# Attention feeding a gated feed-forward block: attention matmuls as array tiles, exp and gate phases per batch, one program order

## The chip, the cores and the metric

One core of a Trainium2 chip. The metric is the device time of one execution in microseconds (us). Executions of one kernel mostly lie within 0.7% of each other. The engines are named as in the profile: PE is TensorE (matmuls), ACT is ScalarE, DVE is VectorE, POOL is GpSimd, which also issues all loads here; PEld is the loading of weights on TensorE. The granted clock is the share of the full TensorE clock that the chip allows at a time.

## The reference, cut to what matters

Eight batches, eight heads, 576 queries, 16 "beacon" keys that everyone sees in front of 576 causal keys, head size 64. The result, 4608 tokens of 512, goes through a gated block of width 1536.

```python
k_all = concat([beacon_k, k]); v_all = concat([beacon_v, v])
a = softmax(0.125 * q @ k_all.T, causal mask on the last 576 keys)
x = (a @ v_all).transpose(0, 2, 1, 3).reshape(4608, 512)
out = (gelu(x @ w_gate) * (x @ w_val)) @ w_out
```

## The kernel before

Heads are handled in pairs, so one 128-row tile holds both. Scores come out transposed (keys on rows). Value matmuls use the exp tile as the stationary operand and give 65 columns, the last of them the row sum. One unit of feed-forward work is put between the key tiles.

```python
# scores: full 128 rows; the other head's half of the queries is zero
nc.tensor.matmul(scs[hi][0:kr, 0:width], kT_sb[0:P, jj*P : jj*P+kr],
                 qT_sb[hi][0:P, s_lo : s_lo+width], start=True, stop=not diag)
...  # diagonal tile: add the mask with an identity matmul, then Exp per head
nc.tensor.matmul(x_ps[0:N, hi, :], expT[0:kr, hi, off : off+N], v_sb[0:kr, jj, 2*m+hi, :], ...)
...  # reciprocal, scale, transpose back into xT_sb
# main loop
for jj in range(N_KT):
    attn_qk_tile(jj, qT_sb, kT_sb, expT)
    try_emit_ffn(tokens_written, 1)
    if pending: attn_av_chunk(*pending.pop(0))
...
```

In the feed-forward part the gate goes through Tanh on ACT and two DVE instructions; every product of 128x512 is one matmul, 1296 of them.

The softmax here doesn't subtract the row's maximum and nothing guards it: scores larger than these inputs give would overflow.

## Time and profile before

| | before |
|---|---|
| time, median of 2 | 484.74 us (484.02 to 485.46) |
| PE busy | 433.9 us of 481.2 |
| one batch of attention and one 512-token chunk | 51.1 us |

First the page: busy time, share of the span and instruction count of PE, then rows of the 40-slice view (tenths busy; PEclk is the granted clock in tenths).

```profile
PE 433.9 (90%) x3384; PEld 238.6 (50%) x3440; DVE 267.6 (56%) x1020; ACT 265.9 (55%) x625; POOL 125.0 (26%) x174
PE   2488699999998999989999999999998999999994
PEclk9999899999999999999999999999999999999998
```

The table of stages of the same kernel: stretch, its length, then busy us (and instructions) of PE, PEld, DVE, ACT and POOL, granted clock, DMA share and GB/s.

```profile
80.00:440.00 360.00, 344.02 (x2736) 189.91 (x2783) 214.50 (x829) 209.49 (x497) 66.17 (x86) 1.00 0.47 46
```

The chain of waits of the same kernel (start, length, what): the first output matmuls of chunks (the third is left out).

```profile
88.09 2.32 PE o_ps L334 x10
...
138.30 2.59 PE o_ps L334 x12
...
241.28 2.59 PE o_ps L334 x12
```

PE is what bounds the kernel from 80 us on: 344 of 360 us busy, at full clock. A chunk and a batch take 51.1 us ((241.28 - 88.09)/3). Twelve 128x512 matmuls take 2.59 us, so the 144 of a chunk take 31.1 us, and four pairs of attention the other 20.0.

### The profile page before, as it was taken

The numbers are of one execution on the slowest core, as the hardware profiler recorded it, in microseconds if no ns is written. First come the engines' busy times: TensorE is split into PE (matmuls) and PEld (weight loads), VectorE is DVE, ScalarE is ACT, GpSimd is POOL, SyncE is SP. The second block draws the span as 40 slices with busy tenths as digits, with TensorE's granted clock in tenths as the row PEclk, the third lists the DMA queues.
The fourth block names the chain that finished last, engine by engine and source line by source line (L and its number), as shares of the span: only waits on it lengthen the run. The fifth ranks groups of instructions, "written<-read, shape, count | busy, mean of one in ns | idle before, by whom it ended". The sixth has DMA issues, their size and how long they took to land.

```text
span 481.2 us, 8884 instructions
## 1 busy us (share of the span) xinstructions
PE 433.9 (90%) x3384; PEld 238.6 (50%) x3440; DVE 267.6 (56%) x1020; ACT 265.9 (55%) x625; POOL 125.0 (26%) x174
## 2 busy tenths in 40 slices
PE   2488699999998999989999999999998999999994
PEld 0255455555555555555555455555555554544441
DVE  0056387347843786268625783488437762782850
ACT  2388546665556755584657556655566554332321
POOL 9998129933430415040330300000000000000000
PEclk9999899999999999999999999999999999999998
DMA  4999999998592809054392800200020000200202
GB/s 28 85 119 163 206 173 126 131 157 52 36 67 80 59 2 101 0 111 29 24 78 89 52 1 0 89 1 1 1 89 1 1 0 1 90 0 1 87 1 87
DMA packets 122491, 29.16 MB, mean 61 GB/s; under 512 B 115280, under 2 KB 116816, under 8 KB 122448
## 3 DMA queue, kind: packets, MB, share of 16 engines
q0 software_dynamic: 117696, 19.15, 54.3%
q1 hardware_dynamic: 4752, 9.44, 5.2%
q8 instruction: 27, 0.44, 0.4%
q14 instruction: 16, 0.13, 0.1%
HBM read 38.27 MB, written 9.44 MB: 99 GB/s over the span
## 4 chain that ended last, share of the span: by engine, by line
PE 66%; ACT 13%; POOL 8%; DVE 6%; DMA 4%; issue 2%; ACTq 0%; POOLq 0%
PE o_ps L334 19%; PE g_ps L297 17%; PE v_ps L306 15%; ACT expT L222 4%; DVE p_sb L316 4%; DMA wv_sb<-in_moe_w_val_dram 4%; PE x_full L240 4%; ACT th_sb L314 4%; POOL v_sb L118 3%; POOL k_sb L118 3%; POOL q_sb L118 2%; PE xTf L261 1%; ACT qT0B_121 L176 1%; ACT kT_sb L188 1%; DVE hT_sb L319 1%
## 5 line engine op out<-in xcount | busy, mean ns | idle before, releaser
L297 PE MATMUL g_ps<-xT_sb,wg_sb 128*128 128x512 bf16 x394 | 109.2, 379 | 7.7 <-DMA wg_sb<-in_moe_w_gate_dram 2.3
L306 PE MATMUL v_ps<-xT_sb,wv_sb 128*128 128x512 bf16 x421 | 111.0, 379 | 1.3 <-DMA wv_sb<-in_moe_w_val_dram 0.9
L314 ACT ACTIVATE th_sb<-g_ps 128x512 bf16<-128x512 f32 x108 | 64.4, 598 | 78.4 <-PE g_ps L297 53.8
L316 DVE SCALAR_TENSOR_TENSOR p_sb<-th_sb,g_ps 128x512 bf16<-128x512 bf16 x108 | 74.1, 687 | 51.7 <-ACT th_sb L314 51.5
L334 PE MATMUL o_ps<-wo_sb,hT_sb 128*128 128x512 bf16 x426 | 98.0, 379 | 0.9 <-DVE xT_sb L262 0.6
L249 DVE RECIPROCAL rec_sb<-x_full 128x1 f32<-128x1 f32 (+2 forms) x320 | 36.5, 155 | 99.0 <-PE x_full L240 84.7
L251 DVE TENSOR_SCALAR xn_sb<-x_full,rec_sb 128x64 bf16<-128x64 f32 (+2 forms) x320 | 76.1, 278 | 0.0
L319 DVE SCALAR_TENSOR_TENSOR hT_sb<-p_sb,v_ps 128x512 bf16<-128x512 bf16 x108 | 73.2, 679 | 4.3 <-PE v_ps L306 2.5
L306 PEld LDWEIGHTS <-wv_sb 128*128 128x128 bf16 x432 | 41.6, 98 | 47.9 <-DMA wv_sb<-in_moe_w_val_dram 1.4
L297 PEld LDWEIGHTS <-wg_sb 128*128 128x128 bf16 x432 | 41.2, 97 | 47.6 <-issue 13.7
L334 PEld LDWEIGHTS <-hT_sb 128*128 128x128 bf16 x432 | 40.6, 98 | 46.0 <-issue 1.6
L240 PE MATMUL x_full<-v_sb,expT 128*128 128x65 bf16 (+3 forms) x960 | 60.4, 198 | 0.0
L240 PEld LDWEIGHTS <-expT 128*128 128x128 bf16 (+3 forms) x960 | 51.0, 108 | 17.7 <-issue 0.6
L341 ACT COPY o_sb<-o_ps 128x512 f32<-128x512 f32 x36 | 21.1, 585 | 68.4 <-PE o_ps L334 68.4
L262 DVE COPY xT_sb<-xTf 128x128 bf16<-128x128 bf16 (+2 forms) x160 | 34.4, 215 | 41.9 <-PE xTf L261 41.9
L118 POOL DMA_DIRECT2D q_sb<-in_q_dram x45 | 37.4, 893 | 47.5 <-PE qT_ps L170 47.5
L118 POOL DMA_DIRECT2D k_sb<-in_k_dram x45 | 37.4, 900 | 16.3 <-DMA wo_sb<-in_moe_w_out_dram 8.3
L216 PEld LDWEIGHTS <-ident 128*128 128x128 bf16 (+1 forms) x320 | 29.6, 103 | 17.7 <-issue 7.7
L261 PE MATMUL xTf<-ident,xn_sb 128*128 128x128 bf16 (+2 forms) x160 | 34.8, 217 | 2.6 <-DVE xn_sb L251 2.2
L118 POOL DMA_DIRECT2D v_sb<-in_v_dram x45 | 37.0, 869 | 0.0
L206 PEld LDWEIGHTS <-kT_sb 128*128 128x128 bf16 (+1 forms) x384 | 33.1, 104 | 6.3 <-issue 3.5
L261 PEld LDWEIGHTS <-xn_sb 128*128 128x128 bf16 (+2 forms) x160 | 15.6, 97 | 27.6 <-DVE xn_sb L251 17.0
(1121 smaller groups left out, 488.2 us busy)
## 6 DMA issues: line engine op xcount, KB each, us to landing
out_dram<-o_sb SPq DMA_DIRECT2D x9, 1024.0 KB, 4.4
q_sb<-in_q_dram POOLq DMA_DIRECT2D x28, 128.0 KB, 5.8
k_sb<-in_k_dram POOLq DMA_DIRECT2D x21, 128.0 KB, 4.4
v_sb<-in_v_dram POOLq DMA_DIRECT2D x21, 128.0 KB, 4.8
wg_sb<-in_moe_w_gate_dram POOLq DMA_DIRECT2D x1, 1536.0 KB, 11.5
wv_sb<-in_moe_w_val_dram POOLq DMA_DIRECT2D x1, 1536.0 KB, 18.1
wo_sb<-in_moe_w_out_dram POOLq DMA_DIRECT2D x1, 1536.0 KB, 26.1
k_sb<-in_k_dram POOLq DMA_DIRECT2D x7, 112.0 KB, 4.6
```

The lines of the kernel that those rows point to most:

```text
L118: nc.gpsimd.dma_start(out=out_ap, in_=in_ap)
L240: nc.tensor.matmul(x_ps[0:N, hi, :], expT[0:kr, hi, off : off + N], v_sb[0:kr, jj, 2 * m + hi, :], start=(idx == 0), stop=(idx == ntiles - 1),
L249: nc.vector.reciprocal(rec_sb[0:N, hi : hi + 1], x_ps[0:N, hi, 64:65])
L251: nc.vector.tensor_scalar(out=xn_sb[0:N, 64 * hi : 64 * hi + 64], in0=x_ps[0:N, hi, 0:64], scalar1=rec_sb[0:N, hi : hi + 1], scalar2=None, ...
L261: nc.tensor.transpose(xT_ps, xn_sb[0:N, :], ident[0:N, 0:N])
L262: nc.vector.tensor_copy(xT_sb[:, m, n0 : n0 + N], xT_ps)
L297: nc.tensor.matmul(g_ps, wg_sb[:, kk, fi * P : (fi + 1) * P], xT_sb[:, kk, n0 : n0 + N_TOK_CHUNK], start=(kk == 0), stop=(kk == K_CHUNKS - 1),
L306: nc.tensor.matmul(v_ps, wv_sb[:, kk, fi * P : (fi + 1) * P], xT_sb[:, kk, n0 : n0 + N_TOK_CHUNK], start=(kk == 0), stop=(kk == K_CHUNKS - 1),
L314: nc.scalar.activation(th_sb, g_ps, ACT.Tanh, scale=GELU_TANH_SCALE)
L316: nc.vector.scalar_tensor_tensor(out=p_sb, in0=th_sb, scalar=1.0, in1=g_ps, op0=ALU.add, op1=ALU.mult)
L319: nc.vector.scalar_tensor_tensor(out=hT_sb[:, fi, :], in0=p_sb, scalar=0.5, in1=v_ps, op0=ALU.mult, op1=ALU.mult,)
L334: nc.tensor.matmul(o_ps, hT_sb[:, fi, ti * P : (ti + 1) * P], wo_sb[:, fi, :], start=(fi == 0), stop=(fi == F_TILES - 1),)
```

## The change

The intent: let PE run two heads side by side (scores on two row halves of the array, values and row sums on two column halves), drop the transposes of x and the mask matmuls, give ACT and DVE fewer and larger instructions, and use the exact Gelu. The kernel loads one table set for Exp and Ln and another for Gelu (16 loads in its trace, 1 in that of the kernel before), so each batch has an exp phase, with the previous chunk's output matmuls filled in, and a gate/value phase. Everything is pinned in program order (`keep`).

```diff
-    scores on 128 rows with zero halves, mask matmul, 12 Exps per pair
+    r = slice(64 * hi, 64 * hi + 64)
+    mm(s_ps[:, hi, col : col + w], qkT[r, 1, t*P : (t+1)*P], qkT[r, 0, s_lo : s_lo + w], True, True)
+    ...
+    act(expT[:, :, o : o + w], s_ps[:, :, 0:w], ACT.Exp, scale=QK_SCALE)   # 4 per pair
+    keep(nc.gpsimd.affine_select(out=d, in_=d, ...))                        # mask, on Pool
-    values: 65 columns, exp tile stationary; reciprocal, scale, transpose, copy
+    mm(x_ps[64*hi : 64*hi+64, base+q0 : base+q1],
+       v_sb[0:kr, t, 2*m+hi, :] if base == X0 else ones[0:kr, :], expT[0:kr, hi, ...], ...)
+    act(ln_sb, x_ps[:, Z0 : Z0 + S], ACT.Ln)
+    act(rec_sb, ln_sb, ACT.Exp, scale=-1.0)
+    keep(nc.vector.tensor_tensor(out=xT_sb[:, m, ...], in0=x_ps[:, X0 : X0 + S], in1=rec_sb, op=ALU.mult))
+    psum_s bufs=2 (scores, transposes, gate/value), psum_x bufs=1, psum_o bufs=1
...
+    for b in range(B):
+        keep(nc.scalar.preload_act_table_set(SET_EXP))
+        for m in range(NPAIR):
+            n = 3 if m < NPAIR - 1 else 2
+            scores(b, m, 0); o(n)                  # o(n): n output matmuls of chunk b-1
+            scores(b, m, 1); av(m - 1, 0, 2); o(n)
+            scores(b, m, 2)
+            if m < NPAIR - 1: transpose_pair(b, m + 1)
+            av(m - 1, 4, 1, 3)
+            scores(b, m, 3)
+            if m: normalize(b, m - 1)
+            o(2 * n if m < NPAIR - 1 else 0)
+            if b == 0 and m < 3: (gate/value weights 1, weights 2, load_batch(1))[m]
+        av(NPAIR - 1, *AV_ORDER); normalize(b, NPAIR - 1)
+        if b + 1 < B: transpose_pair(b + 1, 0)
+        o(8)
+        keep(nc.scalar.preload_act_table_set(SET_GELU))
+        for fi in range(F_TILES):
+            gate_val(b, fi)
+            if fi == 0:
+                if b == 0: load_out_w(); load_batch(2)
+                if b + 3 < B: load_batch(b + 3)
...
```

(Several lines of the diff are joined or cut here.) In `out_mms`, each group of 12 output matmuls ends with a DVE copy of `o_ps`, which has one buffer.

## The prediction

> **What bounds the kernel now.** TensorE. The page gives PE 433.9 us busy of 481.2 (90%); DVE 56%, ACT 55%. In the table of stages PE is 94 to 97% busy from 80 to 440 us; the only poor part is the first 60 us (35.6 us busy), where Pool issues 51 loads one by one (the Pool timeline runs without a gap from 1.8 to 46.8 us). In the chain of waits the output matmuls of successive 512-token chunks start at 88.1, 138.3, 189.8, 241.3, 292.4 us: one chunk and one batch of attention take 51.3 us.
>
> **Terms, from the trace.** Twelve 128x512 matmuls take 2.59 us, so 0.216 us each. The feed-forward part has 1296: 280 us, unchanged. Per chunk that is 31.1 us, so four head pairs of attention cost 20.2 us of the 51.3.
>
> **Removed:** the mask matmuls, the zero-padded halves of the score matmuls, 160 transposes of x with copies, DVE reciprocal and scale (36.5 + 76.1 us), DVE copy of x (34.4), Tanh's extra DVE step (74.1), small ACT instructions (four wide Exps per pair for twelve). DVE and ACT become much lighter, but neither is the limit.
>
> **Added on PE:** values and row sums stream 2x1664 columns per head instead of 65-column matmuls that cost only about 0.04 us each. If the column tiles run in pairs this is 1.4 us per pair plus small-matmul overhead (1.6 to 2.1 us, estimate), scores 0.8, transposes 0.6: about 3 to 3.5 us per pair, against about 4 of issue time now. The Trainium skill, "TensorEngine Tiling (Array Packing)", Key Properties, says a change of tiling mode drains the array; no view of before shows it. There are some ten changes per pair; I take 0 to 0.12 us each.
>
> **Moved, and decisive.** In the exp phase everything stands in program order, o_ps and x_ps have one buffer, and VectorE gets the normalizing multiply before the o_ps copy. Each pair ends: last scores, Exp (0.52), Ln (0.65), Exp (0.65), multiply (0.76), o_ps copy (0.6), about 3.6 us with latencies (sizes scaled from the 598 ns and 687 ns for 512 elements), against 1.7 us of PE work to cover it. I expect PE to wait about 2 us twice per batch for the o_ps copy, and about 3 us before the fourth pair's values. Exp phase: 31 to 36 us per batch; gate/value phase 20.8 us (PE-bound, Gelu and multiply hide). So the period is 52 to 57 us against 51.3: the PE saving is given back as waits.
>
> **Ends.** The first gate phase starts at about 57 us (51.8 before): the mask selects now queue on Pool behind 17 loads of the next batch at 0.8 us each. Batch 1 may lose 5 us to the same queue. Tail after the eighth gate phase: 31 + 10.4 + 5 us.
>
> Sum: 57 + 20.8 + 7 x 53 + 46 = 495 us. **Predicted 495 us, 460 to 530.** Faster 0.24, same 0.28, slower 0.48.
>
> **What would show it.** PE busy falls to 75 to 80%; PE idle before the first output matmul of pairs 2 and 3 released by the o_ps copy (about 2 us each), and before the fourth pair's value matmuls released by the multiply (3 us); gate phases of 20.8 us with PE full; two value matmuls on different column halves starting within a few ns; in batch 0, value matmuls waiting for Pool's selects; Pool below its former share late, busy early.
>
> **What would make it wrong.** If column tiles do not overlap, add 1.4 us per pair (45 us). If mode changes are free and the waits are shorter than I estimate, the period falls to 46 us and the time to 445. Extra table loads between Exp and Ln would add 1.28 us each (the one load in the trace).

## The result, and the profile after

525.18 us (524.96 to 525.40, 2 runs) against 484.74: slower, ratio 1.084 (95% interval 1.080 to 1.088). Ratios in this document are not quite the ratios of the medians quoted.

The page of the changed kernel, the same lines:

```profile
PE 421.1 (80%) x3104; PEld 208.2 (40%) x3152; DVE 147.0 (28%) x214; ACT 233.4 (45%) x316; POOL 185.1 (35%) x326
PE   2373796869976998779887988699769977899985
PEclk9996699899999899979998999899999999799999
```

PE has fallen from 90% to 80% of a longer span. DVE went from 267.6 to 147.0 us and ACT from 265.9 to 233.4: savings on engines that were not the limit. The PEclk row has more and deeper dips (down to 6) than before, where it has one 8 and the end.

The chain of waits, with the first long piece of successive gate/value phases:

```profile
119.81 9.06 PE gv_ps L132 x42
...
175.41 9.06 PE gv_ps L132 x42
...
232.19 9.06 PE gv_ps L132 x42
...
287.79 9.06 PE gv_ps L132 x42
```

From one to the next it is 55.6, 56.8 and 55.6 us (mean of six periods up to 453.47: 55.6) against 51.1 before. The table of stages for one gate/value phase and one exp phase (columns as above):

```profile
119.80:140.80 21.00, 20.89 (x98) 9.30 (x98) 8.30 (x12) 6.80 (x12) 6.51 (x9) 1.00 0.92 69
140.80:175.40 34.60, 26.44 (x277) 14.28 (x280) 8.30 (x12) 21.41 (x27) 14.59 (x29) 0.95 0.35 42
```

The gate/value phase is full of PE work. The exp phase has 26.4 us of PE work in 34.6 us. Where the other 8 us go is seen in the timeline at the end of one pair (start, length, engine, instruction, and in brackets the idle time before it and what ended it; here and below, weight loads and other lines that the reading does not need are left out):

```profile
264.49 0.26 PE L132 MATMUL s_ps<-qkT_110 64*128 64x208 bf16 x2
264.69 1.47 PE L132 MATMUL o_ps<-wo_sb,hT_sb 128*128 128x512 bf16 x6
264.80 0.52 ACT L135 ACTIVATE expT<-s_ps 128x416 bf16<-128x416 f32 x1 [0.66 <-PE s_ps L132]
265.21 0.64 ACT L135 ACTIVATE ln_sb<-x_ps 128x576 f32<-128x576 f32 x1
265.88 0.68 ACT L135 ACTIVATE rec_sb<-ln_sb 128x576 f32<-128x576 f32 x1
266.09 0.39 PE L132 MATMUL s_ps<-qkT_108 64*128 64x512 bf16 x2
...
266.60 0.76 DVE L223 TENSOR_TENSOR xT_sb<-x_ps,rec_sb 128x576 bf16<-128x576 f32 x1 [2.01 <-ACT rec_sb L135]
267.27 0.68 DVE L272 COPY o_sb<-o_ps 128x512 f32<-128x512 f32 x1
268.01 0.81 PE L132 MATMUL o_ps<-wo_sb,hT_sb 128*128 128x512 bf16 x3 [1.53 <-DVE o_sb L272]
```

The six output matmuls have been done since 266.16, so the copy of `o_ps` could run from then on. But the multiply stands before it in program order and waits for Exp, Ln and Exp on ACT: DVE stays idle for another 0.44 us (the last part of its 2.01 us), then multiplies, and the copy starts at 267.27, 1.1 us late. PE, which has done the first scores of the next pair meanwhile, waits 1.53 us for the copy. The waits of PE in the changed kernel that matter here (total us, times, longest):

```profile
PE o_ps L132 <- DVE o_sb L272: 28.1, 25, 1.5
PE x_ps L132 <- DVE xT_sb L223: 22.0, 9, 2.7
PE x_ps L132 <- POOL expT L180: 14.4, 3, 10.2
...
PE s_ps L132 <- ACT expT L135: 6.1, 18, 0.7
...
PE t_ps L146 <- ACT expT L135: 3.4, 7, 0.5
```

The second line is the fourth pair, whose value matmuls wait 2.66 us for the multiply that frees `x_ps`. The third is mostly one wait in batch 0, in the timeline there:

```profile
50.79 4.19 POOL L108 DMA_DIRECT2D v_sb_102<-in_v_dram  x5 [0.37 <-issue]
54.95 1.76 POOL L180 TENSOR_SCALAR_AFFINE_SELECT expT<-expT 128x224 bf16<-128x224 bf16 x5
55.43 0.69 PE L132 MATMUL x_ps<-expT,v_sb_98 128*64 128x496 bf16 x4 [10.21 <-POOL expT L180]
```

Pool issues all 17 loads of batch 1 before the mask selects that the fourth pair needs. The last two lines of the waits are for the most part the table load at the start of each exp phase, in the timeline of batch 4:

```profile
252.94 0.60 ACT L135 ACTIVATE ge_sb<-gv_ps 128x512 bf16<-128x512 f32 x1 [1.13 <-PE gv_ps L132]
253.56 1.28 ACT L294 ACT_TABLE_LOAD   x1
254.85 2.72 ACT L135 ACTIVATE expT<-s_ps 128x1024 bf16<-128x1024 f32 x3
255.93 0.37 PE L132 MATMUL s_ps<-qkT_108 64*128 64x464 bf16 x2 [0.47 <-ACT expT L135]
256.79 0.42 PE L146 MATMUL t_ps<-ident,q_sb_100 128*128 128x128 bf16 x5 [0.49 <-ACT expT L135]
```

And the table of stages around the 2.66 us wait of that batch shows a cost that no wait shows: the granted clock (the number before the last two).

```profile
279.50:282.20 2.70, 0.06 (x2) 0.00 (x0) 0.76 (x1) 1.82 (x4) 2.34 (x4) 1.00 0.00 0
282.20:283.20 1.00, 0.98 (x12) 0.68 (x14) 0.00 (x0) 0.00 (x0) 1.00 (x2) 0.64 1.23 79
283.20:284.20 1.00, 1.00 (x18) 0.86 (x16) 0.00 (x0) 0.00 (x0) 1.00 (x3) 0.50 1.54 98
284.20:285.20 1.00, 1.00 (x17) 0.79 (x14) 0.00 (x0) 0.17 (x1) 1.00 (x2) 0.50 1.79 114
285.20:286.20 1.00, 0.94 (x11) 0.88 (x10) 0.00 (x0) 0.97 (x2) 1.00 (x3) 0.65 2.35 150
```

After the wait PE works for about 3.4 us at half clock, which loses 0.36 + 0.50 + 0.50 + 0.35 = 1.7 us. That an idle PE falls to half clock is in the Trainium skill, "TensorE: Matmul & The Clock Gate", Part 1; it speaks of idle windows of about 3.4 us, and here 2.66 us were enough. They were not always: in this profile six of the seven waits of 2.66 us were followed by half clock (about 3.4 us four times, 6.8 us twice), in the control's profile (e0) five of seven, in that of e1 four. None of the fourteen waits of 1.53 us was, within 5 us. The kernel before has one such case, after a wait of 2.28 us.

### The profile page after: what moved, and what is told of

The parts are those of the page before. It is cut to its first block, busy times and chain, and to the rows that moved or that the text cites. A ratio compares the mean times of both kernels' runs of the same rounds, so it can differ in the third digit from the quotient of the medians.

```text
span 523.7 us, 7515 instructions
## 1 busy us (share of the span) xinstructions
PE 421.1 (80%) x3104; PEld 208.2 (40%) x3152; DVE 147.0 (28%) x214; ACT 233.4 (45%) x316; POOL 185.1 (35%) x326
## 4 chain that ended last, share of the span: by engine, by line
PE 62%; ACT 12%; POOL 11%; DVE 5%; DMA 5%; issue 4%; DVEq 0%; POOLq 0%
PE gv_ps L132 32%; PE o_ps L132 13%; PE x_ps L132 11%; ACT expT L135 5%; PE s_ps L132 4%; DVE o_sb L272 3%; PE t_ps L146 3%; ACT rec_sb L135 3%; POOL v_sb_98 L108 2%; DMA wo_sb<-in_moe_w_out_dram 2%; ACT ln_sb L135 2%; POOL k_sb_97 L108 2%; DMA wv_sb<-in_moe_w_val_dram 2%; DVE xT_sb L223 2%; POOL q_sb_96 L108 2%
## 5 line engine op out<-in xcount | busy, mean ns | idle before, releaser
L135 ACT ACTIVATE expT<-s_ps 128x1024 bf16<-128x1024 f32 (+3 forms) x128 | 108.5, 864 | 96.3 <-PE s_ps L132 95.8
L180 POOL TENSOR_SCALAR_AFFINE_SELECT expT<-expT 128x256 bf16<-128x256 bf16 (+2 forms) x160 | 59.9, 404 | 252.2 <-ACT expT L135 251.3
L132 PE MATMUL o_ps<-wo_sb,hT_sb 128*128 128x512 bf16 x401 | 106.5, 388 | 32.9 <-DVE o_sb L272 28.1
L135 ACT ACTIVATE ge_sb<-gv_ps 128x512 bf16<-128x512 f32 x108 | 64.5, 597 | 137.3 <-PE gv_ps L132 137.3
L132 PE MATMUL gv_ps<-xT_sb,wg_sb 128*128 128x512 bf16 x422 | 110.7, 380 | 0.6 <-issue 0.2
L132 PE MATMUL gv_ps<-xT_sb,wv_sb 128*128 128x512 bf16 x425 | 109.4, 379 | 0.4
L251 DVE TENSOR_TENSOR hT_sb<-gv_ps,ge_sb 128x512 bf16<-128x512 f32 x108 | 74.7, 692 | 123.2 <-ACT ge_sb L135 123.2
L132 PE MATMUL x_ps<-expT,ones 128*64 128x144 bf16 (+5 forms) x576 | 54.2, 275 | 0.0
L132 PE MATMUL x_ps<-expT,v_sb_98 128*64 128x80 bf16 (+5 forms) x216 | 21.1, 284 | 20.6 <-POOL expT L180 11.9
L272 DVE COPY o_sb<-o_ps 128x512 f32<-128x512 f32 x36 | 24.7, 685 | 21.4 <-PE o_ps L132 21.4
L132 PE MATMUL s_ps<-qkT_108 64*128 64x512 bf16 (+2 forms) x192 | 23.4, 295 | 8.5 <-ACT expT L135 5.3
L132 PEld LDWEIGHTS <-ones 128*64 128x64 bf16 (+1 forms) x576 | 27.1, 127 | 6.4 <-issue 1.5
L132 PE MATMUL x_ps<-expT,v_sb_102 128*64 128x80 bf16 (+5 forms) x216 | 19.7, 272 | 10.5 <-DVE xT_sb L223 8.0
L132 PE MATMUL s_ps<-qkT_110 64*128 64x512 bf16 (+2 forms) x192 | 23.3, 297 | 0.8 <-ACT expT L135 0.8
```

Of the source, the lines that this page charges most:

```text
L132: keep(nc.tensor.matmul(out_ap, lhsT, rhs, start=start, stop=stop, **kw))
L135: keep(nc.scalar.activation(out_ap, in_ap, func, **kw))
L180: nc.gpsimd.affine_select(out=d, in_=d, pattern=[[0, 2], [1, DIAG[t]]], compare_op=ALU.is_ge, fill=0.0, base=NB if t == 0 else 0, channel_ ...
L251: nc.vector.tensor_tensor(out=h_of[ci][:, fi, :], in0=gv_ps[:, 1, :], in1=ge_sb, op=ALU.mult)
L272: keep(nc.vector.tensor_copy(o_sb[:, ti, :], o_ps))
```

## The experiments

My theory after the result: the PE work did get shorter, and the program order gave it back in separate waits. The rival: PE's own work is what got long (tiles that do not overlap, or changes of tiling), and the waits only show slack. Each of the first three runs mends one wait. Unless said otherwise an edit is to the changed kernel, whose time as a control was 525.47 us (4 runs; ratio to before 1.082). The experiments ran on three chips (e1 to e4, e5 to e8, the rest). The kernel before ran in each, with medians of 484.87, 484.39 and 485.49 us, so the ratios compare best, and a difference of medians between calls carries about 1 us of that.

### e1_copy_first

```diff
-            if m:
-                normalize(b, m - 1)
             o(2 * n if m < NPAIR - 1 else 0)
+            if m:
+                normalize(b, m - 1)
```

> Edit: the output matmuls that end a pair are written before the normalization, so VectorE copies o_ps before it does the normalizing multiply. Theory (waits on single-buffered PSUM tiles in program order eat the gain): the two waits of 1.53 us per batch before the next pair's output matmuls shrink to about 0.6 us (o_ps copy starts when the sixth matmul lands), the multiply comes 0.3 us later and hurts nobody; 2.1 us x 7 batches = 15 us less, about 510 us. Rival (TensorE's own work is longer than thought: tiling changes, small matmuls, cold clock): the wait moves to another place and the time stays within 3 us of 525.

Measured: 507.11 us (4 runs), ratio to before 1.045, so 18 us less than the control. PE's wait for the copy fell from 28.1 to 13.2 us in all; in the timeline the 1.53 us became:

```profile
258.30 0.81 PE L132 MATMUL o_ps<-wo_sb,hT_sb 128*128 128x512 bf16 x3 [0.46 <-DVE o_sb L272]
```

The order of two DVE instructions cost 3.5% of the kernel. The rival of this run fell. The waits account for 15 of the 18 us. Part of the rest is clock: after its seven waits of 2.66 us PE was at half clock for 17 us in all in the profile of e1 and for 24 us in the control's, which is worth up to 3.4 us. Whether the edit or chance did that is not shown.

### e2_fill_fourth

```diff
+        o(8)
         av(NPAIR - 1, *AV_ORDER)
         normalize(b, NPAIR - 1)
         if b + 1 < B:
             transpose_pair(b + 1, 0)
-        o(8)
```

> Edit: the eight output matmuls that follow the fourth pair's value matmuls are put before them, into the 2.66 us wait for the normalizing multiply. Theory: the wait falls to about 0.9 us, the TensorE clock stays granted in full and the 36 value matmuls take 2.1 us where they took 2.8; a new wait of about 1.1 us appears at the start of the gate phase, which now has less work to hide the last normalization. Net about 1.3 us x 7 = 9 us less, about 516 us. Rival (the wait is only where slack shows, and the gate phase waits for the whole amount): within 2 us of 525.

Measured: 511.02 us (4 runs), ratio 1.054, 14 us less than the control where I expected 9. The two waits, before the fourth pair's values and at the start of the gate phase, came as foreseen:

```profile
275.18 0.44 PE L132 MATMUL x_ps<-expT,v_sb 128*64 128x496 bf16 x4 [0.83 <-DVE xT_sb L223]
...
279.06 0.38 PE L132 MATMUL gv_ps<-xT_sb,wg_sb 128*128 128x512 bf16 x1 [0.97 <-DVE xT_sb L223]
```

And the same stretch in the table of stages:

```profile
274.30:281.00 6.70, 4.90 (x60) 2.94 (x59) 2.83 (x5) 3.25 (x5) 6.70 (x10) 1.00 1.52 130
```

By waits alone the gain is 2.66 - 0.83 - 0.97 = 0.9 us per batch. The rest is clock: between 274.3 and 281.0 us it is granted in full (1.00), and the mean over the run rose from 0.951 in the profile of the changed kernel to 0.979. No half clock follows any of these waits in the profile of e2, so it was the long wait that brought it. Covering a wait of 2.7 us was worth about 2 us per batch.

### e3_load_order

```diff
-            if b == 0 and m < 3:
-                (weights 1, weights 2, load_batch(1))[m]
+            if b == 0 and m != 2:
+                (weights 1, weights 2, None, load_batch(1))[m]
...
-        if b + 1 < B:
+        if b + 1 < B and b > 0:          # batch 1: after gate_val(0, 6)
             transpose_pair(b + 1, 0)
...
-                if b == 0: load_out_w(); load_batch(2)
-                if b + 3 < B: load_batch(b + 3)
+                if b == 0: load_out_w()
+                if b + 2 < B: load_batch(b + 2)
```

> Edit: the loads of batch 1 are issued after the fourth pair's mask selects of batch 0 (its first transposes move into the gate phase), and each gate phase issues one batch of loads, two ahead, where the first one issued two. Theory (Pool issues loads in program order ahead of the selects): the 10.2 us wait before the fourth pair's value matmuls of batch 0 goes to about 1.5 us, so the first gate phase starts at about 50.5 us in place of 59.3; the wait of 2.55 us for a select and the cold stretch behind it in batch 1 go (5 us). Together 13.5 us less, about 512 us. Rival (the start is bound by the transfers themselves): the first gate phase still starts near 57 us and the gain is under 4 us.

Measured: 513.51 us (4 runs), ratio 1.059, 12 us less than the control. The first gate phase started at 50.8 us in place of 59.3, and PE's waits for Pool's selects fell from 14.4 to 1.6 us. The first gate matmuls of the changed kernel, then of this run:

```profile
59.31 0.63 PE L132 MATMUL gv_ps<-xT_sb,wg_sb 128*128 128x512 bf16 x1
...
50.84 1.17 PE L132 MATMUL gv_ps<-xT_sb,wg_sb 128*128 128x512 bf16 x3
```

The loads were not late because transfers were slow; they stood in front of the selects in Pool's queue.

### e4_no_table

```diff
-        act(ge_sb, gv_ps[:, 0, :], ACT.Gelu)
+        act(ge_sb, gv_ps[:, 0, :], ACT.Exp)      # wrong result on purpose
-        keep(nc.scalar.preload_act_table_set(SET_EXP))      # and SET_GELU
+        if b == 0: keep(nc.scalar.preload_act_table_set(SET_EXP))
```

> Wrong on purpose: Gelu is replaced by Exp, which is in the table set of the exp phase, so no table is switched (1 load in place of 17); every instruction has the same size. Theory: in the first pair of each batch TensorE waits 1.1 us for Exps that are late by the 1.28 us load, so 7 x 1.1 = 8 us less, about 517 us; I left this term out of the prediction. Rival (the loads are hidden): within 2 us of 525.

Measured: 520.48 us (516.85 to 523.94, 4 runs), ratio 1.073 (1.067 to 1.079) against 1.082 (1.079 to 1.086) for the control. Some 5 us, less than the 8 expected and with the widest scatter of all runs. In its timeline the three waits for Exp in the first pair (0.47, 0.49, 0.15 us) are down to one of 0.35, so 0.76 us per batch. (The trace of the changed kernel has 16 table loads, not the 17 of the expectation.) The table switches are on the path, but a small part.

### e5_serial_cols

```diff
-        for base, split in ((X0, 496), (Z0, 432)):
+        for hi, base, split in ((0, X0, 496), (0, Z0, 432), (1, X0, 496), (1, Z0, 432)):
             for q0, q1 in ...:
-                for hi in range(2):
```

> Edit to the changed kernel: the value and row-sum matmuls of one pair are ordered all of the first head, then all of the second, so that neighbours write the same column half and cannot run side by side; the work is the same. Theory (the column tiles of two heads overlap, as the trace suggests: four matmuls of 1152 columns in all start and stream within 0.27 us): each pair then takes 2.77 us of streaming in place of 1.39, and as these matmuls lie on the chain of every pair, about 1.4 us x 32 = 40 us more, 555 to 570 us. Rival (they did not overlap, or the order does not matter): within 5 us of 525.

Measured: 523.13 us (519.72 and 526.55), ratio 1.080: no change. The expectation failed, and not because there was no overlap. The timeline of PE in a window of 0.1 us:

```profile
272.38 0.41 PE L132 MATMUL x_ps<-expT,v_sb 128*64 128x496 bf16 x2
```

Both 496-column matmuls start within about 0.02 us (one takes 0.397, the two together 0.41), though three matmuls of the first head stand between them in the order of the kernel; the trace does not show whether the compiler kept that order. They start 0.013 us apart, where as neighbours in the changed kernel they start 0.003 us apart. PE ran them side by side all the same, so this edit did not take the overlap away. e9 does.

### e6_before_rowtiled (one part of the change alone, in the kernel before)

```diff
-        nc.scalar.copy(qTA0[0:64, :], qT_ps[0:64, 0:S])
-        nc.scalar.copy(qT0B[64:128, :], qT_ps[64:128, 0:S])
+        nc.scalar.copy(qT, qT_ps[:, 0:S])
...
-                    kT_sb[0:P, jj * P : jj * P + kr],
-                    qT_sb[hi][0:P, s_lo : s_lo + width],
+                    kT_sb[64 * hi : 64 * hi + 64, jj * P : jj * P + kr],
+                    qT_sb[64 * hi : 64 * hi + 64, s_lo : s_lo + width],
```

> Edit to the kernel BEFORE: one part of the change alone, the scores of the two heads as row tiles (64 rows each, one copy of the transposed queries without zero halves); all else as it was. Theory (TensorE is what bounds that kernel, so TensorE work taken away there does shorten it): 1664 fewer streamed columns per pair, 0.69 us, less some 0.1 us for each change of tiling, about 0.3 us net x 32 = 10 us less, about 474 us, at least 5 us less than before. Rival (the tiling changes cost as much as the overlap saves): within 3 us of before or slower.

Measured: 501.20 us (5 runs), ratio to before 1.033: slower by 17 us, where the rival said within 3 us of before or slower. PE starts of the kernel before, scores of 464 columns and the masks that follow:

```profile
200.06 0.36 PE L206 MATMUL sc_3179<-qTA_1_120,kT_sb 128*128 128x464 bf16 x1
200.26 0.36 PE L206 MATMUL sc_3180<-qT0B_121,kT_sb 128*128 128x464 bf16 x1
200.45 0.22 PE L216 MATMUL sc_3179<-mb_std,ident 128*128 128x128 bf16 x1
```

The same spot of this run:

```profile
214.92 0.37 PE L204 MATMUL sc<-qT_sb,kT_sb 64*128 64x464 bf16 x2
215.22 0.29 PE L214 MATMUL sc<-mb_std,ident 128*128 128x128 bf16 x2
```

Two scores of 464 columns took 0.39 us before. Now they stream together, in about 0.19 us (an estimate, half of it), but the next matmul starts only after 0.30 us: a gap of 0.1 us at the change from half rows to all rows. A pair has up to 12 such changes here, so by this gap (an estimate) some 1.2 us for a saving of 0.69, a loss of 0.5 us per pair or 2 us per batch. The stretches between first output matmuls show half of that: the four at full clock take 52.7, 51.4, 53.1 and 50.4 us, 51.9 in the mean, against 50.9 in the mean of six before, so 1 us per batch. The Trainium skill, "TensorEngine Tiling (Array Packing)", Key Properties, says that a change of tiling mode drains the array; this trace shows a gap at the change, and its size.

The rest of the 17 us looks like clock. The first output matmul comes 8 us later than before (96.06 for 88.09). The PEclk row shows 9 up to there, but the trace has no record of the clock before 64 us; the length of a mask matmul tells. In the kernel before it is 0.31 us at first and 0.22 from 25.2 us on; in this run it is still 0.29 at 59.3 us and 0.23 from 65 us on:

```profile
25.20 0.22 PE L216 MATMUL sc_275<-mb_std,ident 128*128 128x128 bf16 x1
...
59.27 0.29 PE L214 MATMUL sc<-mb_std,ident 128*128 128x128 bf16 x1
...
215.69 0.23 PE L214 MATMUL sc<-mb_std,ident 128*128 128x128 bf16 x1
```

The profiled execution (505.19 us, the slowest of the five) has two more stretches of 6.8 us at half clock, with no wait of PE over 0.9 us before them. Why the clock stayed low is not shown. So this run shows a cost of the tiling changes of about 1 us per batch more than they save, and not the whole 17 us.

### e7_three (e1, e2 and e3 together)

> The three mended waits together (copy first, out matmuls before the fourth pair's values, load order). Theory: they are different waits in different places, so the gains add: 525 - 18 - 14 - 12 = 481 us, within 5 us, so just level with the kernel before. Rival (one bottleneck stands behind all of them): the sum is less than two thirds of that, over 496 us.

Measured: 486.05 us (4 runs), ratio to before 1.002 (1.000 to 1.005). The three gains sum to 18 + 14 + 12 = 44 us and together gave 39, so the time lies just outside the expected 481 within 5. They are in the main separate waits, not one bottleneck; why some 5 us overlap is not shown.

### e8_best (the same work, another order)

```diff
+            for m in range(NPAIR):                     # b > 0
+                scores(b, m, 0);  if m == 0: o(9)
+                scores(b, m, 1);  if m == 0: o(3)
+                av(m - 1, 0, 2);  if m == 2: o(3)
+                scores(b, m, 2);  av(m - 1, 4, 1, 3)
+                if m < NPAIR - 1: transpose_pair(b, m + 1)
+                if m == 0: o(3)
+                if m: normalize(b, m - 1)              # ahead of the pair's last Exp
+                scores(b, m, 3);  if m: o(9)
+            av(NPAIR - 1, *AV_ORDER); normalize(b, NPAIR - 1)
+            if 0 < b < B - 1: transpose_pair(b + 1, 0)
+            o(3)
...  # batch 0: heads 0-3 loaded first; values of heads 4-7 and the weights issued
...  # between the selects; load_batch(b + 2) in gate phase b
...  # last chunk: o_ps alternates with a slice of the free x_ps
```

> The changed kernel with its work unchanged and its order redone: out matmuls spread so that every wait on o_ps, x_ps and the table load is covered (15, 9, 12 and 12 in the four pairs), normalization queued before the last Exp of a pair, batch 0 loaded four heads at a time with its mask selects between the loads, loads two batches ahead, and the last chunk's outputs alternate between two PSUM tiles. Theory (nothing but order made the change slow): the first gate phase starts at about 44 us, an exp phase takes 26 to 28 us in place of 34.6, TensorE busy over 90%; about 440 us, 430 to 455. Rival (the tiled matmuls carry a cost of their own beyond waits): no better than 470 us.

Measured: 447.68 us (447.39 to 448.09, 4 runs), ratio to before 0.924 (0.922 to 0.926): 7.6% faster than the kernel before and 15% faster than the changed one, with the same operations. PE is busy 403.0 us of 446.4 (90%). The chain of waits, starts of two gate/value phases:

```profile
98.94 9.66 PE gv_ps L133 x44
...
145.71 9.66 PE gv_ps L133 x44
```

The period is 46.8 us in place of 55.6; the first gate phase starts at 45.0 us (44 expected). What made the change slow was its order, given one buffer each for `o_ps` and `x_ps`, which e8 keeps except in the last chunk. The main rule of the new order: a group of 12 output matmuls ends where PE has scores, values or transposes to do next, so the copy of `o_ps` has time.

### e9_untiled_values and e10_untiled_scores (what the tiles are worth when PE is the limit)

Both undo one tiling in e8, with results wrong (the heads are summed). The check does not see this error.

```diff
# e9: one stationary operand of 128 columns for both heads
-                        x_ps[64 * hi : 64 * hi + 64, base + q0 : base + q1],
-                        v_sb[0:kr, t, 2 * m + hi, :] if base == X0 else ones[0:kr, :],
+                        x_ps[:, base + q0 : base + q1],
+                        v_sb[0:kr, t, 2 * m : 2 * m + 2, :] if base == X0 else ones[0:kr, :],
# e10
-                r = slice(64 * hi, 64 * hi + 64)
+                r = slice(0, P)
```

> Wrong on purpose (the two heads' results are summed): the reordered kernel e8, in which TensorE is 90% busy so that TensorE time shows in the total, with the value and row-sum matmuls as full 128-column matmuls, the same number and the same columns streamed by each, but no column tiles, so no two can run side by side. Theory (column tiles of two heads overlap; the run with another order of heads only failed to part them): 1.39 us more streaming per pair less two changes of tiling of 0.1 us, 1.2 us x 30 = 35 us more, 475 to 490 us. Rival (there is no overlap to lose, which would also explain why the other order changed nothing): within 5 us of 448.

Measured: 482.89 us (4 runs), ratio to before 0.996: 35 us more than e8. The column tiles do overlap, and their net worth is 35/32 = 1.1 us per pair. The second theory of e5, that there was no overlap to lose, is out.

> Wrong on purpose (scores summed over both heads): the reordered kernel e8 with every score matmul on all 128 rows, so no row tiles. Theory (each change of tiling costs about 0.1 us, which is what ate the saving in the kernel before with row-tiled scores): 0.69 us more streaming per pair, less 5 to 7 changes of tiling saved, 0.5 to 0.7 us: within 6 us of 448 us. Rival (tiling changes are free, and the loss in the other run had another cause): 0.69 x 30 = 20 us more, about 468 us.

Measured: 454.41 us (4 runs), ratio 0.936: 6.7 us more than e8 by the medians, just outside my 6, and 5.9 by the ratios (0.9361 - 0.9240 of 485; the two ran on different chips); far from the rival's 20. The period grew from 46.8 to 47.4 us, 0.15 us per pair where 0.69 us more is streamed, so about 0.5 us came back, as the theory has it from changes of tiling that were no longer made. Row-tiled scores gain a little in a schedule with few changes of tiling, and lost about 1 us per batch in one with many (e6).

### e0_changed (control)

> The changed kernel as it was given, as a control on the same chip: 525 us within 2 us. It is the measure for the runs of the two earlier calls that came out close to it (the serial order of heads and the kernel without table switches).

Measured: 525.47 us (523.63 to 526.78, 4 runs), ratio to before 1.082.

## Why the prediction was right or wrong

The direction was right (0.48 for slower, the largest chance, but about even odds) and 525 us lies inside 460 to 530. The size was wrong: 495 us is 10 us over the kernel before, and the change cost 40.

What held:
- The mechanism. "I expect PE to wait about 2 us twice per batch for the o_ps copy, and about 3 us before the fourth pair's values": measured 1.53 us twice and 2.66 us. The runs e1 and e2 show that these waits set the time.
- Gate/value phases of 20.8 us with PE full: 20.89 of 21.00 us busy.
- The queue on Pool in batch 0 and 1, shown by e3.
- Tiles that overlap, about ten changes of tiling per pair at 0 to 0.12 us each: e9 shows the overlap, and e10 fits about 0.1 us a change.

What failed is the sum, "57 + 20.8 + 7 x 53 + 46", and in it above all the step that priced the exp phase. The same terms measured are 59.3 + 20.8 + 60.5 + 6 x 55.6 + 49.4 = 523.6 us:
- The period, taken as 53 us, was 55.6, 16 us over six batches. Less 20.8 us for the gate/value phase, 53 leaves 32.2 us for the exp phase. The prediction's own terms for it (10.4 us of output matmuls, four pairs of 3 to 3.5, 7 us of waits) give only 29.4 to 31.4; I had written 52 to 57 for the period and took a value below the middle. Measured between 140.8 and 175.4 us: 24.7 us of PE work as at full clock, 5.7 us of the waits that I did foresee (2 x 1.53 + 2.66, less than the 7), and two costs that were missing. PE works at half clock for about 3.4 us after the long wait (1.7 us lost; e2 gave back more than its waits). And 2.4 us of other waits: 1.1 behind the table load, of which e4 got back 0.76, 0.46 for the `o_ps` copy after the first pair, the rest small.
- Batch 1 took 60.5 us. "Batch 1 may lose 5 us to the same queue" stood in the text and not in the sum; it lost 60.5 - 55.6 = 4.9 us.
- The start (59.3 for 57) and the tail (49.4 for 46) add the last 6 us. In the tail the four groups of output matmuls wait 1.14 us and then three times 0.78 us for the copy of the one before.

## What to carry to other kernels

When work is taken off the engine that is the limit, look at what its instructions wait for in program order: with a single buffer, the copy that frees it must not stand behind an instruction that waits for another engine's chain. Add up every wait you name, and for long ones price the half clock that may follow: here most waits of 2.66 us brought it and none of 1.53 us did. Tiling the array paid here where matmuls of one tiling stay together (e8 to e10); between short runs of other matmuls its 0.1 us per change can eat the gain (e6).

## What the Trainium skill lacked or had wrong

- "TensorEngine Tiling (Array Packing)", Key Properties: names the drain at a change of tiling mode but gives no size. Here a gap of about 0.1 us per change (0.30 us from start to start where two overlapping matmuls stream for an estimated 0.19 us), enough to turn the saving of row-tiled scores into a loss of about 1 us per batch in e6.
- "TensorE: Matmul & The Clock Gate", Part 3, The mechanism: says that matmuls start in strict program order. In e5, two matmuls on different column halves, with three others between them in the order of the kernel, started 0.013 us apart, and the first of the three began only 0.22 us later. The trace does not show whether the compiler kept the kernel's order.
- "TensorE: Matmul & The Clock Gate", Part 1: gives about 3.4 us of idling before the clock halves. Here six of the seven waits of 2.66 us in the changed kernel were followed by a granted clock of 0.50, and in the kernel before one of 2.28 us was, while none of the fourteen of 1.53 us was (1.00).
- "ScalarE: Activation LUTs", What ACT_TABLE_LOAD costs: gives 2.66 us for a switch, half of it a drain. The trace shows 1.28 us of load, with the next Exp 0.01 us after its end and the load 0.02 us after the last Gelu; no run here shows the drain.
